# ConvNeXt-V2 block on one core: the expansion 13 instead of 14 slots behind the convolution

## The chip, the core and the metric

The kernel runs on one core of a Trainium2 chip. The core has five engines with a queue of instructions each: TensorE (PE, with its weight loads shown as PEld), VectorE (DVE), ScalarE (ACT), GpSimd (POOL) and SyncE (SP), which here only issues DMAs. Each queue is worked off in order; engines wait for one another by semaphores. The metric is the time of one execution in microseconds on the device. The time before is 1430.02 us, the median of three runs (1429.26 to 1431.42).

## What is computed

One block of a vision network on an image of 512 x 512 pixels and 96 channels, bfloat16:

```python
out = sum over i, j of xp[:, i:i+H, j:j+W, :] * dw[i, j]     # 3 x 3 depthwise convolution
h = layernorm(out)                                           # over the 96 channels of a pixel
h = gelu(einsum('bhwc,ce->bhwe', h, w1))                     # 96 -> 384: the expansion
gx = sqrt((h * h).sum(axis=(1, 2)) + 1e-6)                   # per channel, over the whole image
nx = gx / (gx.mean(axis=-1) + 1e-6)
h = grn_gamma * (h * nx) + grn_beta + h
return x + einsum('bhwe,ec->bhwc', h, w2)                    # 384 -> 96
```

The sum of squares in `gx` needs the whole image before the last product can begin. So there are two phases: the first makes the sums, the second the output.

## The kernel before

The image is cut into 128 blocks of four rows. The first phase runs in slots; `put` (line 842) enters in a table what is done for which block in which slot, and the loop from line 884 issues each slot's work engine by engine, in an order written out by hand. All engines used here are wrapped so that they keep the program's order (`InOrder`, line 26).

In slot s the block s is convolved: 72 small matmuls on PE in three bursts (`conv_taps`), which read x transposed by DVE (`turn_x`, three slots ahead) from tiles that SP loads five slots ahead (`load_x`, four buffers). ACT copies the result to `y_bf` (`evac`), DVE a third of it in some slots ("shared"). A square `ysq` follows (`stage_sq`, on POOL where the slot has an expansion, on ACT where it has none), and in slot s + 2 PE sums both over the channels (`stage_stats`).

Layer norm's factor is made for batches of four blocks. With L the slot of the last sums of a batch: `stage_moments` (DVE) in L scales the sums and clears them with a memset; `stage_rstd` (four small POOL operations) in L + 1; `stage_newton` (six more) and `stage_turn` (a DVE transposition of the result) in L + 2; `stage_rows` (two DMAs to DRAM) in L + 3; `stage_bcast` (four DMAs of 128 KB from there to all partitions, tile `rbc`) in L + 4. From slot L + 5 on one block a slot is multiplied (`stage_norm`, POOL, tile `yn`, three buffers). If the norm is in slot s, the four DMAs of `stage_write` to DRAM are issued in s + 1, the read back in another layout (`stage_read`, tile `ynT`) in s + 2, and the expansion is in s + 4: matmuls with w1, gelu on ACT into `g`, and the sum of squares, for some quarters by DVE (`bn_stats`, function `entry`), for the others by PE as a gram matrix (`gram_next`). The gram matrix and the sums of `stage_stats` share one PSUM bank.

The expansion of a block thus lies 14 slots behind its convolution. Slots 0 to 4, 7 and 10 to 17 have a convolution and no expansion, slots 18 to 127 have both, and slots 128 to 141 have an expansion alone (`mlp_tail`, 14 blocks from `TAIL0` on). 36 blocks are "whole": their `g` is stored to DRAM in three parts (`store_next`, one part a slot). Eight are held in SBUF for the second phase, in `gpool` or in tiles that the convolution no longer needs (`IN_XT`, `IN_XIN`, `IN_GH`). The rest are expanded a second time in the second phase (from line 1116), which multiplies by w2, adds x and writes the output.

SP's order within a slot from slot 20 on (lines 887 to 908): load of x, rows, broadcast, reads, writes, one store of `g`. POOL's: Newton steps, square, norm, rstd (lines 909 to 916).

Of the kernel before, what the change touches and what calls it, by code (L numbers as in the profile page):

```python
# [17 lines left out]
FILL = (6, 15)  # L18
BATCH = 4
WHOLE = (0, 3, 7)  # L20
NTAIL = 14
GRB = 3
PORTION = 4

# [33 lines left out]
def kernel(  # L58
# [30 lines left out]
    r_dram = dram.tile([NBLK, GR, W], bf16, name="r_dram")  # L89

    TAIL0 = NBLK - NTAIL
    HELD = [TAIL0 + i for i in (2, 3, 4, 6, 7, 9, 10, 11)]
    KEPT = [NBLK - 6, NBLK - 2, NBLK - 1]
    IN_XT, IN_XIN, IN_GH = (TAIL0, TAIL0 + 4), TAIL0 + 9, TAIL0 + 11

    def is_held(q):
        return q in HELD

    def is_whole(q):
        return q < TAIL0 and q % 10 in WHOLE or q == TAIL0  # L100

    def after_whole(q):
        return (q - 1) % 10 in WHOLE
# [99 lines left out]
    with ExitStack() as p1:  # L203
# [352 lines left out]
        def stage_moments(k):  # L556
            N = BATCHES[k][1] * GR * NG
            m = small.tile([128, 2, NS], f32, name="mom")
            dve.tensor_scalar(out=m[:, :, :N], in0=S[:, :, :N], scalar1=1.0 / C, scalar2=None, op0=ALU.mult)
            dve.memset(S[:], 0.0)  # L560
            msts[k] = m
# [134 lines left out]
        def quarter(b, t):  # L696
            return gs[b][t] if isinstance(gs[b], list) else gs[b][:, t]
# [9 lines left out]
        def mlp_tail(b, get):  # L707
            if b == IN_GH:
                gs[b] = late.gh.tile([128, NQ, NCH, QW], bf16, name="gh")[:]
            elif b > IN_GH:  # L710
                gs[b] = late.gr.tile([128, NQ, NCH, QW], bf16, name="gr")[:]
            elif b in IN_XT:
                gs[b] = g_xt
            elif b == IN_XIN:
                gs[b] = g_xin
            elif not is_held(b):
                while len(sums_only) < 2 * NQ:
                    sums_only.append(ypool.tile([128, NCH, QW], bf16, name="y_bf")[:])
                gs[b] = sums_only[:NQ]
                sums_only.extend(sums_only[:NQ])  # L720
                del sums_only[:NQ]
            else:
                gs[b] = gpool.tile([128, NQ, NCH, QW], bf16, name="g")[:]
            for t in range(NQ):
                cm = t < cm_quads(b)
                (cm_unit if cm else px_unit)(quarter(b, t), ynts[b], t)
                gram_next(12 if len(grams) > 24 else 6)
                if cm:
                    for j in range(NCH):
                        entry(b, j, t)  # L730
                if t == 1:
                    for k in get("turn"):
                        stage_turn(k)
                if t == 2:
                    for b2 in get("stats"):
                        stage_stats(b2)
                if t > cm_quads(b):
                    owe_grams(b, (t - 1) * QC, t * QC)
            for k in get("moments"):
                stage_moments(k)  # L740
            if cm_quads(b) < NQ:
                owe_grams(b, (NQ - 1) * QC, NQ * QC)
            if is_whole(b):
                stores.extend((b, h) for h in range(3))
# [63 lines left out]
        def gram_next(n):  # L808
            for b, c0, j in grams[:n]:
                c = c0 % QC + j * 128  # L810
                v = quarter(b, c0 // QC).rearrange("p j w -> p (j w)")[:, c:c + 128]
                pe.matmul(gram[:, j, :], lhsT=v, rhs=v, start=False, stop=True, skip_group_check=True)
            del grams[:n]
# [28 lines left out]
        def put(s, what, v):  # L842
            at.setdefault((s, what), []).append(v)

        RAMP = 4
        AHEAD = 20
        HOLE = 10
        LATE = 26
        last_norm = -1
        mlp_slots = set()  # L850
        for k, (b0, n) in enumerate(BATCHES):
            for b in range(b0, b0 + n):
                on_act = b not in mlp_slots
                put(b if on_act else b + 1, "sqa" if on_act else "sqp", b)
                last_s = b + 1 if b < RAMP else b + 2
                put(last_s, "stats", b)
            ramp = b0 + n <= RAMP
            if ramp:
                put(last_s, "chain", k)
                put(last_s + 1, "spread", k)  # L860
            else:
                put(last_s, "moments", k)
                put(last_s + 1, "rstd", k)
                put(last_s + 2, "newton", k)
                put(last_s + 2, "turn", k)
                put(last_s + 3, "rows", k)
                put(last_s + 4, "bcast", k)
            for b in range(b0, b0 + n):
                last_norm = s = max(last_norm + 1, last_s + (1 if ramp else 5))
                put(s, "norma" if ramp else "norm", b)  # L870
                put(s + 1, "write", b)
                put(s + 2, "read", b)
                m = s + (3 if ramp else 4)
                mlp_slots.add(m)
                put(m, "mlp", b)
                put(m + is_whole(b), "combine", b)
                last_slot = m
# [5 lines left out]
        turn_x(2)  # L883
        for s in range(last_slot + 1):
            get = lambda kind: at.get((s, kind), [])
            early = s < AHEAD
            if s < HOLE:
                for b in get("read"):
                    stage_read(b)
            while loaded[0] < min(s + 6, NBLK):  # L890
                load_x(loaded[0])
                loaded[0] += 1
            if HOLE <= s and early:
                for b in get("read"):
                    stage_read(b)
            for k in get("rows"):
                stage_rows(k)
            for k in get("bcast"):
                stage_bcast(k)
            if not early:  # L900
                for b in get("read"):
                    stage_read(b)
            for b in get("write"):
                stage_write(b)
            if not HOLE <= s < HOLE + 8:
                store_next()
            if any(b >= TAIL0 for b in get("mlp")):
                store_next()
            for k in get("newton"):
                stage_newton(k, pool)  # L910
            for b in get("sqp"):
                stage_sq(b, False)
            for b in get("norm"):
                stage_norm(b)
            for k in get("rstd"):
                stage_rstd(k, pool)
            mlp = get("mlp")

            def spread_out(bank=0):
                for k in get("spread"):  # L920
# [1 line left out]
                for b in get("norma"):  # L922
                    stage_norm(b, dve if b < 2 else pool)

            spare = not mlp and s % 2 == 1
            taps, evac = conv_taps(s, spare) if s < NBLK else ([], None)
            if mlp and mlp[0] >= TAIL0:
                assert not taps
# [36 lines left out]
            else:  # L965
                b = mlp[0]
# [32 lines left out]
                if not shared:  # L999
                    squares(2)  # L1000
                    gram_next(PORTION)
                if s >= LATE:
                    for k in get("turn"):
                        stage_turn(k)
                conv(2, u4)
                if evac:
                    evac(shared)
# [16 lines left out]
                    stage_moments(k)  # L1024
                squares_rest(2)
                square_owed()
                if s < LATE:
                    for k in get("turn"):
                        stage_turn(k)
                if is_whole(b):  # L1030
                    owed.append(lambda f=squares_rest: f(3))
                owe_grams(b, cm_quads(b) * QC, NQ * QC)
                if is_whole(b):
                    stores.extend((b, h) for h in range(3))
            if s == 0:
                setup_ynt()
            if s == 4:
# [129 lines left out]
```

## Time and profile before

The page of the profiled execution and the answers of its trace give:

| | us |
|---|---|
| profiled execution | 1432.47 |
| its span | 1429.7 |
| median of the three timed runs | 1430.02 |
| busy: ACT | 1379.6 (96%) |
| busy: PE | 1377.3 (96%) |
| busy: DVE | 1306.8 (91%) |
| busy: POOL | 888.8 (62%) |
| last evacuation of a convolution | at 857.83 |
| first instruction of the second phase's outputs on DVE | at 944.87 |

How to read it: the share over the whole span is an average over two phases with different work. POOL, for instance, has nothing but DMA issues in the second phase and is busy most of the first. So the stretches are read one by one. In a line of the timeline the columns are start, duration (of a merged group: from the first start to the last end), engine, line, operation, output and input tile, count, and in brackets the idle time before it with what ended it. All instructions that a wrapped engine issues have line 36 of the kernel, so they are told apart by their tiles. "SPq" is SP's queue of DMA issues; such an instruction ends when the DMA is issued, not when it has landed.

### The profile page before, as it was taken

The page shows a single profiled execution, that of the slowest core. Times are in us where ns is not written, and L with a number is a line of the kernel's source. Part 1 is how long each engine was busy: PE and PEld are TensorE (multiplying, and loading weights), DVE is VectorE, ACT ScalarE, POOL GpSimd, SP SyncE. Part 2 cuts the span into 40 slices and gives each one's busy share as a digit, 9 for nine tenths or more (in the row PEclk, how much of TensorE's full clock was granted, in tenths as well). Part 3 has the DMA queues.
Part 4 walks back from the last instruction along what each step waited for, and adds up shares of the span by engine and source line. Part 5 has one row for each costly group of instructions (what it writes and reads, how often), then busy time and mean ns, then how long its engine had stood idle before and what let it go on. Part 6 is the DMA issues. An engine that isn't in the chain of part 4 may idle for free.

```text
span 1429.7 us, 55018 instructions
## 1 busy us (share of the span) xinstructions
PE 1377.3 (96%) x23332; PEld 826.7 (58%) x23332; DVE 1306.8 (91%) x2400; ACT 1379.6 (96%) x1693; POOL 888.8 (62%) x735
## 2 busy tenths in 40 slices
PE   8989999999999999999999997799999999999998
PEld 3444555545555555555545554367777777777776
DVE  8958999999999999999999999988888888888888
ACT  7889999999999999999999999999999999999997
POOL 3559999999999999999999997302111111111110
PEclk9999999999999999999999999999999999999999
DMA  6568999898988998889888978649999999999996
GB/s 177 189 175 259 272 277 279 264 292 240 271 262 276 274 283 264 276 261 272 250 263 270 260 229 261 204 161 405 419 378 389 403 414 389 408 393 415 412 405 259
DMA packets 167565, 423.65 MB, mean 296 GB/s; under 512 B 34166, under 2 KB 83766, under 8 KB 162710
## 3 DMA queue, kind: packets, MB, share of 16 engines
q1 hardware_dynamic: 151652, 314.59, 68.9%
q0 software_dynamic: 15104, 105.39, 18.5%
q8 instruction: 182, 2.98, 0.9%
q14 instruction: 65, 0.53, 0.1%
q10 hardware_dynamic: 562, 0.15, 0.1%
HBM read 262.16 MB, written 157.79 MB: 294 GB/s over the span
## 4 chain that ended last, share of the span: by engine, by line
PE 51%; ACT 19%; DVE 17%; DMA 7%; issue 2%; SPq 2%; POOL 1%; ACTq 0%; POOLq 0%; DVEq 0%
PE PS L36 51%; ACT g L36 14%; DVE bst L36 10%; ACT y_bf L36 4%; DVE xT L36 3%; DVE o_sb L36 2%; DMA out_dram<-o_sb 2%; DMA yn_dram<-yn 2%; SPq L36 2%; DMA ynT<-yn_dram 1%; DMA xin<-in_x_dram 1%; DVE y_bf L36 1%; DMA rbc<-r_dram 1%; POOL ysq L36 1%; ACT xT L36 1%
## 5 line engine op out<-in xcount | busy, mean ns | idle before, releaser
L36 ACT ACTIVATE g<-PS 128x512 bf16<-128x512 f32 (+2 forms) x1160 | 703.7, 777 | 6.5 <-PE PS L36 6.1
L36 DVE BATCH_NORM_STATS2 bst<-g 128x6 f32<-128x512 bf16 x1020 | 623.4, 675 | 23.1 <-ACT g L36 22.3
L36 ACT ACTIVATE gr<-PS 128x1536 bf16<-128x1536 f32 x344 | 479.8, 1457 | 14.8 <-PE PS L36 8.6
L36 POOL TENSOR_TENSOR yn<-y_bf,rbc 128x1536 bf16<-128x1536 bf16 x126 | 391.6, 3110 | 55.5 <-DMA rbc<-r_dram 22.3
L36 PE MATMUL PS<-ynT,w1p 128*128 128x512 bf16 x1110 | 341.1, 380 | 22.1 <-ACT g L36 7.7
L36 PE MATMUL PS<-xT,Wq 64*32 64x511 bf16 (+1 forms) x9198 | 336.3, 386 | 7.8 <-ACT y_bf L36 1.0
L36 DVE TENSOR_TENSOR o_sb<-PS,B2c 128x384 bf16<-128x384 f32 x512 | 280.6, 556 | 58.8 <-PE PS L36 53.1
L36 POOL TENSOR_TENSOR ysq<-y_bf 128x1536 bf16<-128x1536 bf16 x114 | 313.4, 2750 | 25.0 <-ACT y_bf L36 17.7
L36 PEld LDWEIGHTS <-g 128*128 128x128 bf16 (+1 forms) x3603 | 217.5, 98 | 117.9 <-issue 35.4
L36 PE MATMUL PS<-ynT,w1s 128*128 128x512 bf16 x972 | 262.6, 379 | 0.2 <-issue 0.2
L295 POOL DMA_DIRECT2D xr<-in_x_dram x116 | 62.4, 538 | 286.4 <-DVE o_sb L36 286.4
L36 PEld LDWEIGHTS <-gr 128*128 128x128 bf16 x4104 | 200.9, 98 | 53.6 <-issue 1.8
L36 PE MATMUL PS<-W2s,gr 128*128 128x96 bf16 x4032 | 209.7, 206 | 1.0 <-DVE o_sb L36 0.4
L36 ACT ACTIVATE y_bf<-PS 128x1536 bf16<-128x1536 f32 (+2 forms) x147 | 182.5, 1264 | 14.1 <-PE PS L36 13.0
L36 PEld LDWEIGHTS <-w1p 128*128 128x128 bf16 x1110 | 94.8, 97 | 163.7 <-issue 109.7
L36 DVE STREAM_TRANSPOSE xT<-xin 128x576 f32<-128x576 f32 (+1 forms) x256 | 181.8, 751 | 6.1 <-PE PS L36 6.1
L36 PEld LDWEIGHTS <-Wq 64*32 64x32 bf16 x9216 | 104.6, 90 | 127.0 <-ACT g L36 56.5
L36 PE MATMUL PS<-g 128*128 128x128 bf16 x1632 | 157.8, 219 | 3.8 <-DVE PS L36 3.2
L36 DVE TENSOR_TENSOR o_sb<-o_sb,xr 128x768 bf16<-128x768 bf16 x256 | 142.8, 558 | 8.9
L36 PE MATMUL PS<-w1p,ynT 128*128 128x384 bf16 (+1 forms) x924 | 141.6, 273 | 7.4 <-ACT xT L36 2.1
L36 PEld LDWEIGHTS <-ynT 128*128 128x128 bf16 x924 | 73.0, 97 | 59.5 <-issue 37.1
L36 PE MATMUL PS<-W2s,g 128*128 128x96 bf16 x1968 | 103.9, 206 | 0.7 <-DVE o_sb L36 0.4
(114 smaller groups left out, 659.8 us busy)
## 6 DMA issues: line engine op xcount, KB each, us to landing
g<-g_dram POOLq DMA_DIRECT2D x36, 1536.0 KB, 9.8
xin<-in_x_dram SPq DMA_DIRECT2D x126, 432.0 KB
g_dram<-g SPq DMA_DIRECT2D x105, 512.0 KB
yn_dram<-yn SPq DMA_DIRECT2D x512, 96.0 KB
ynT<-yn_dram SPq DMA_DIRECT2D x128, 384.0 KB
out_dram<-o_sb SPq DMA_DIRECT2D x127, 384.0 KB
xr<-in_x_dram POOLq DMA_DIRECT2D x124, 384.0 KB, 7.5
ynT<-yn_dram SPq DMA_DIRECT2D x243, 128.0 KB
```

Of the source, the lines that this page charges most:

```text
L36: r = f(*a, **k)
L295: pq.dma_start(out=xr[:], in_=x[0, r0:r0 + GR].rearrange("r w c -> (r w) c").rearrange("(p g) c -> p g c", g=PXP))
```

## The change

The expansion of a block moves one slot nearer to its convolution. The steps between are put closer together, and several orders within a slot change with it:

- `NTAIL` is 13: the tail begins at block 115, slot 17 has an expansion, and there are 141 slots instead of 142. Block 114 stays whole; its `g` is now in `gpool` instead of the x tiles. The set of held blocks is unchanged.
- rstd, Newton steps, the transposition and the rows are all in slot L + 1, the broadcast in L + 2, the norm from L + 4 on. On POOL, in a slot that has all three, the order is norm, rstd with Newton steps, square; else square, rstd, norm. The transposition and the rows are issued at the slot's end.
- `yn` is written in the slot of its norm and read in the next one. The expansion is still four slots after the norm.
- SP's order in a slot becomes: load of x, reads, broadcast, store of `g`, and behind the norm the writes, then at the end the rows. The slots without a store end at 16 instead of 17.
- In the tail the transposition is at the slot's end instead of behind the second quarter; in the slot with the last moments the sums and the moments come behind the first quarter's matmuls, ahead of its `bn_stats`.
- In the slots from 10 on that have a convolution alone, the even ones instead of the odd ones use the spare banks.

```diff
-NTAIL = 14
+NTAIL = 13
...
-    HELD = [TAIL0 + i for i in (2, 3, 4, 6, 7, 9, 10, 11)]
+    HELD = [TAIL0 + i for i in (1, 2, 3, 5, 6, 8, 9, 10)]
...
-        return q < TAIL0 and q % 10 in WHOLE or q == TAIL0
+        return q < TAIL0 and q % 10 in WHOLE or q == TAIL0 - 1
...
                 (cm_unit if cm else px_unit)(quarter(b, t), ynts[b], t)
+                if t == 0 and get("moments"):
+                    for b2 in get("stats"):
+                        stage_stats(b2)
+                    for k in get("moments"):
+                        stage_moments(k)
...
-                if t == 1:
-                    for k in get("turn"):
-                        stage_turn(k)
-                if t == 2:
+                if t == 2 and not get("moments"):
...
-            for k in get("moments"):
-                stage_moments(k)
+            for k in get("turn"):
+                stage_turn(k)
...
                 put(last_s, "moments", k)
                 put(last_s + 1, "rstd", k)
-                put(last_s + 2, "newton", k)
-                put(last_s + 2, "turn", k)
-                put(last_s + 3, "rows", k)
-                put(last_s + 4, "bcast", k)
+                put(last_s + 1, "turn", k)
+                put(last_s + 1, "rows", k)
+                put(last_s + 2, "bcast", k)
             for b in range(b0, b0 + n):
-                last_norm = s = max(last_norm + 1, last_s + (1 if ramp else 5))
+                last_norm = s = max(last_norm + 1, last_s + (1 if ramp else 4))
                 put(s, "norma" if ramp else "norm", b)
-                put(s + 1, "write", b)
-                put(s + 2, "read", b)
+                put(s + ramp, "write", b)
+                put(s + ramp + 1, "read", b)
...
-            if HOLE <= s and early:
+            if HOLE <= s:
                 for b in get("read"):
                     stage_read(b)
-            for k in get("rows"):
-                stage_rows(k)
             for k in get("bcast"):
                 stage_bcast(k)
-            if not early:
-                for b in get("read"):
-                    stage_read(b)
-            for b in get("write"):
-                stage_write(b)
-            if not HOLE <= s < HOLE + 8:
+            if not HOLE <= s < HOLE + 7:
                 store_next()
             if any(b >= TAIL0 for b in get("mlp")):
                 store_next()
-            for k in get("newton"):
-                stage_newton(k, pool)
-            for b in get("sqp"):
-                stage_sq(b, False)
-            for b in get("norm"):
-                stage_norm(b)
-            for k in get("rstd"):
-                stage_rstd(k, pool)
             mlp = get("mlp")
+            steps = [lambda b=b: stage_sq(b, False) for b in get("sqp")]
+            norms = [lambda b=b: stage_norm(b) for b in get("norm")]
+            roots = [lambda k=k: (stage_rstd(k, pool), stage_newton(k, pool)) for k in get("rstd")]
+            for f in norms + roots + steps if roots and steps and norms else steps + roots + norms:
+                f()
+            for b in get("write"):
+                stage_write(b)
...
-            spare = not mlp and s % 2 == 1
+            spare = not mlp and s % 2 == (1 if s < HOLE else 0)
...
-                if s < LATE:
-                    for k in get("turn"):
-                        stage_turn(k)
+                for k in get("turn"):
+                    stage_turn(k)
...
+            for k in get("rows"):
+                stage_rows(k)
```

More of the change, by code (lines that the diff above doesn't have):

```diff
@@ L91 @@
     TAIL0 = NBLK - NTAIL
-    HELD = [TAIL0 + i for i in (2, 3, 4, 6, 7, 9, 10, 11)]
+    HELD = [TAIL0 + i for i in (1, 2, 3, 5, 6, 8, 9, 10)]
     KEPT = [NBLK - 6, NBLK - 2, NBLK - 1]
-    IN_XT, IN_XIN, IN_GH = (TAIL0, TAIL0 + 4), TAIL0 + 9, TAIL0 + 11
+    IN_XT, IN_XIN, IN_GH = TAIL0 + 3, TAIL0 + 8, TAIL0 + 10
     def is_held(q):
@@ L711, in mlp_tail @@
                 gs[b] = late.gr.tile([128, NQ, NCH, QW], bf16, name="gr")[:]
-            elif b in IN_XT:
+            elif b == IN_XT:
                 gs[b] = g_xt
@@ L845 @@
         RAMP = 4
-        AHEAD = 20
         HOLE = 10
-        LATE = 26
         last_norm = -1
@@ L885 @@
             get = lambda kind: at.get((s, kind), [])
-            early = s < AHEAD
             if s < HOLE:
@@ L1001 @@
                     gram_next(PORTION)
-                if s >= LATE:
-                    for k in get("turn"):
-                        stage_turn(k)
                 conv(2, u4)
@@ L1026 @@
                 square_owed()
-                if s < LATE:
-                    for k in get("turn"):
-                        stage_turn(k)
+                for k in get("turn"):
+                    stage_turn(k)
                 if is_whole(b):
```

## The prediction

> **What bounds the kernel now.** I read the page first, for the busy shares in its 40 slices, then the table of windows, then the waits and the timeline of SP's own DMA queue, because what is moved here is mostly DMA issues.
>
> ```profile
> span 1429.7 us, 55018 instructions
> ...
> ACT  7889999999999999999999999999999999999997
> ```
>
> The slices show one flat stretch, up to about 860 us, in which the convolution of one block and the expansion of an earlier one share a slot. The table of windows says how full it is; its columns are busy us of PE, PEld, DVE, ACT and POOL, clock, DMA share and GB/s.
>
> ```profile
> 200.00:850.00 650.00, 642.88 (x11798) 333.77 (x11796) 636.88 (x1123) 647.75 (x1033) 618.42 (x421) 1.00 0.89 266
> 900.00:925.00 25.00, 17.75 (x117) 9.26 (x117) 23.22 (x40) 25.00 (x20) 6.92 (x3) 1.00 0.59 177
> ```
>
> ACT is busy 647.75 of 650 us, so it sets the pace. On its timeline the evacuation of block 32 starts at 198.96 and that of block 120 at 809.70: 88 slots of 6.94 us, 27.76 us for the four slots of a batch. The others stand close behind. SP is not in that table, and its waits are where I look next: between 200 and 850 us,
>
> ```profile
> SPq L36 <- DMA yn_dram<-yn: 88.3, 116, 3.2
> ```
>
> SP waits for the landing of its own writes of yn: the read of a block may be issued only when that block's four writes are in DRAM. Two loops from SP's timeline (start, duration), the first a plain one, the second with the broadcast of rstd:
>
> ```profile
> 435.83 0.32 SPq L36 DMA_DIRECT2D ynT<-yn_dram  x1
> 436.60 2.52 SPq L36 DMA_DIRECT2D yn_dram<-yn  x4
> 439.16 1.35 SPq L36 DMA_DIRECT2D g_dram<-g  x1
> 440.62 0.37 SPq L36 DMA_DIRECT2D xin<-in_x_dram  x1
> 442.11 0.33 SPq L36 DMA_DIRECT2D ynT<-yn_dram  x1
> ```
>
> ```profile
> 475.06 0.33 SPq L36 DMA_DIRECT2D ynT<-yn_dram  x1
> 475.45 2.58 SPq L36 DMA_DIRECT2D yn_dram<-yn  x4
> 478.13 0.53 SPq L36 DMA_DIRECT2D g_dram<-g  x1
> 478.70 0.44 SPq L36 DMA_DIRECT2D xin<-in_x_dram  x1
> 479.19 2.64 SPq L36 DMA_DIRECT2D rbc<-r_dram  x4
> 481.94 0.36 SPq L36 DMA_DIRECT2D ynT<-yn_dram  x1
> ```
>
> The reader is to see the order: read, writes, store of g, load of x, broadcast, next read. The store, the load and the broadcast stand between the writes and the read that waits for them. In the first loop the read comes 2.99 us after the writes' last issue, 1.12 us of it idle; in the second 3.91 us of issues cover the landing. Over this stretch the plain loops take 6.80 us (read to read, 40 of them), those with a broadcast 7.21, those with the rows of rstd 6.77. A batch is two plain ones and one of each: 27.6 us. SP hardly waits for anything else, so it runs at ACT's pace with nothing to spare.
>
> **The change part by part.** The profiled execution took 1432.47 us, 2.8 us more than its span and 2.45 above the median of 1430.02. I work out differences on its rows and put them on the median.
>
> *One slot fewer.* Slot 17, a convolution alone, takes over the expansion of block 4, and that of block 114 goes from the tail into slot 127. A slot with a convolution alone costs 3.49 us (evacuations at 66.90 and 91.30, seven slots); an expansion alone in the tail 5.38 (fourteen on ACT from 861.04 to 936.40); both together 6.94. Sum: 6.94 - 3.49 - 5.38 = -1.9 us. The square of block 17 goes to POOL (2.75 us; POOL has gaps there, the largest 8.4 us before 102.68).
>
> *rstd whole in one slot.* No instruction is added. POOL's order becomes norm, ten small operations, two squares; before, one square stood in front of the norm. Its four slots cost 4 x 3.07 + 4 x 2.70 + 3.9 = 27.0 us either way, under 27.76. rstd is ready 2.7 us sooner against its slot; the transposition of it is asked for up to a slot sooner, so DVE can wait for POOL there, and behind it stand the transpositions of x and the casts. It did so before, 2.82 us at 85.16 and 1.89 at 109.72. In the steady stretch the evacuation of a slot plus about 1 us is where I put rstd, plus 2.6 us where DVE gets to it: no wait. In the first two batches I allow 2 to 6 us of DVE time, which lies beside ACT work: 0 taken, 4 us as the upper end.
>
> *Rows and broadcast sooner.* The same DMAs. POOL's wait for the broadcast goes, but POOL is not the bound: 0, at best the 3.0 us of ACT waits between 98 and 135 us, for reads that came late after the hole. I take -1.5.
>
> *yn written in its norm's slot, the store ahead of it.* This is the large term. SP's order becomes load of x, read, broadcast, store of g, four writes, rows. Between writes and the read that waits for them only the load of x is left (and the rows in one slot of four); store and broadcast now follow that wait instead of covering it. The chain from read to read is then serial:
>
> - read 0.33 + 0.08 to the next issue = 0.41;
> - store 0.70 + 0.08 = 0.78, in nine slots of ten;
> - writes 2.51 + 0.08 = 2.59;
> - from the writes' last issue to the next read 3.31 (mean of the 40 plain loops, 1.76 to 5.01), which hides the load of x, and the rows' 1.3 us as well.
>
> A plain slot is 7.09 us, one with a broadcast 2.1 more. Four slots: 4 x 7.09 + 2.1 - 0.3 for missing stores = 30.2 us against ACT's 27.76. The landing may get shorter when transfers spread out. The nearest row with less traffic is in the tail, where the DMA share is 0.59 (second window above):
>
> ```profile
> 906.93 2.48 SPq L36 DMA_DIRECT2D yn_dram<-yn  x4
> 911.10 0.31 SPq L36 DMA_DIRECT2D ynT<-yn_dram  x1
> ```
>
> 1.69 us there, 2.07 in the next loop: about 1.9 at 0.59 and 3.31 at 0.89. On a line between them the new share, 0.89 x 27.76/29.4 = 0.84, gives 3.1 us and a batch of 29.4 us. That is 0.41 us a slot too slow. The chain breaks even at a landing of 2.7 us. How an order of this kind runs is seen once before, in slots 17 and 18, where read and broadcast stand ahead of the writes:
>
> ```profile
> 94.29 0.33 SPq L36 DMA_DIRECT2D ynT<-yn_dram  x1
> 94.67 1.82 SPq L36 DMA_DIRECT2D rbc<-r_dram  x4
> 96.53 5.52 SPq L36 DMA_DIRECT2D yn_dram<-yn  x4
> 102.15 0.53 SPq L36 DMA_DIRECT2D xin<-in_x_dram  x1
> 103.90 0.31 SPq L36 DMA_DIRECT2D ynT<-yn_dram  x1
> ```
>
> 9.6 us for a loop without a store, so 9.2 for one with a broadcast is not too high.
>
> The lag is absorbed at first: block 60 is read at 475.06 and expanded from about 486.4 (seven gelus before the evacuation at 490.61), 11.3 us later, of which I leave 4 to the read itself. So 7 us are free, 17 slots at 0.41. From slot 18 to the last load of x in slot 122 there are 105: 88 x 0.41 = +36 us. In the tail SP's loops without load and store (4.5 to 5.3 us) keep up with ACT's 5.38: 0. What is late first is the read of yn, then PE's first matmuls of an expansion, then ACT.
>
> The Trainium skill, *DMA: Bandwidth & Descriptors*, section "Latency and other measured facts", says the receipt from HBM makes most of a DMA's fixed cost, 0.2 us on average and 2 us at high load, less when the load is lighter. The trace agrees in direction (1.69 and 3.31 us). By that rule alone, an estimate, up to 1.8 us of landing could go, and the 36 us would be 0; by the rows they are 36.
>
> *The tail.* Moments ahead of bn_stats, the transposition of rstd at the slot's end. ACT runs from 861.04 to 936.40 without a gap and covers all of it; without that cover it is the 0.5 us of moments and memset. 0 taken. *Where the moments fall.* An expansion is one block further on at each moments slot, and the gram matmuls that waited for the memset (0.90 us at 181.04, six waits of 3.7 us in all) fall elsewhere: -4 to +4, 0 taken.
>
> Sum: -1.9 - 1.5 + 36 + 0 = +33 us, 2.3%: 1430 + 33 = 1463.
>
> **The rivals.**
>
> *Faster: the landing shrinks below 2.7 us.* Its place is SP's wait between the writes and the read. For it: 1.7 to 2.1 us in the tail, and the minimum of 1.76 among the plain loops; SP then never gets 7 us behind. Against: between 824 and 860 us, where no x is loaded any more and the share is 0.81 to 0.82, it is 3.83, 3.33, 1.85 and 2.62 in the four loops without rows or broadcast, 2.9 in the mean. Then only the first terms stay: -1.9 - 1.5, and up to -4 for the gram waits: 1423 to 1428, say 1426. By the rule cited above this one would win; the rows at 0.81 and above speak against that.
>
> *Heavier: the landing stays at 3.31 or the writes wait as at 96.53.* With 30.2 to 31 us a batch: 0.6 to 0.8 us a slot over some 95 slots, +57 to +76, less 3.4: 1484 to 1503.
>
> *No change: SP keeps up, and what the slot gives is taken back by DVE* waiting for rstd after the hole, 4 us at most since DVE then sets ACT back only once: 1427 to 1432, say 1430. The 2.82 us at 85.16 speak for it, DVE's 13 us of slack between 200 and 850 against.
>
> **How the numbers follow.** Chances: the serial chain as worked out 0.55 (landing 2.85 to 3.25 us, 28.4 to 30 us a batch, 1436 to 1483); heavier 0.13; faster 0.22; no change 0.10, of which 0.08 within 0.2% and 0.02 slower. 0.2% is about what a measurement of this kernel can tell from no change. So faster 0.22, same 0.08, slower 0.70. The point is the likeliest case's, 1463. The range leaves out a tenth at each end, the lower half of the faster case and most of the heavier one: 1425 to 1490; the likeliest case's own is 1436 to 1483.
>
> **What would show it.** In SP's timeline of after: read, store, writes, load, read, with a gap of 2 us and more ahead of the reads where there was 1.75; loops of 7 us and more, over 9 with a broadcast; evacuations on ACT more than 7.2 us apart from about slot 35 on, with PE waiting for the read of yn and ACT for PE; ACT's busy share in the stretch down to some 94% and the DMA share to 0.84. It is wrong if ACT stays at 99% there, if the landing falls to 2.7 us or less, or if SP waits for POOL's norm instead. POOL's wait for the broadcast should be gone in any case.

## The result and the profile after

The changed kernel takes 1528.57 us (median of five runs, 1527.89 to 1533.31), the kernel before 1429.26 us beside it (1426.69 to 1431.42): a ratio of 1.0704, 95% interval 1.0685 to 1.0723. It is 99 us slower; 33 were forecast, and the range ended at 1490. Slower was right, and so was the place, but the time lost is three times the sum.

The first two lines below are the span and ACT's slices on the page of the changed kernel, the next two its table of windows, with the same columns as that of before (busy us of PE, PEld, DVE, ACT and POOL, clock, DMA share, GB/s):

```profile
span 1526.2 us, 55022 instructions
...
ACT  7879989899889989998998899799999999999997
```

```profile
200.00:850.00 650.00, 591.33 (x10555) 303.73 (x10553) 573.76 (x1004) 589.13 (x922) 549.45 (x376) 0.97 0.81 239
946.00:1026.00 80.00, 55.20 (x437) 31.05 (x422) 61.98 (x113) 67.66 (x52) 40.07 (x24) 0.89 0.68 206
```

ACT is busy 589.13 of 650 us, 91%, where it was 647.75. No engine is full any more, and the DMA share has fallen from 0.89 to 0.81: something waits in a circle. From the evacuation of block 32 (210.0) to that of block 120 (893.1) a batch of four slots takes 31.05 us instead of 27.76. The second line is the tail, where ACT had no gap before; now it stands still for 12.3 us.

The waits of SP's queue and of all engines, 200 to 850 us:

```profile
SPq L36 <- DMA yn_dram<-yn: 148.6, 171, 4.1
SPq L36 <- DMA ynT<-yn_dram: 15.7, 15, 2.3
```

```profile
POOL yn L36 <- DMA rbc<-r_dram: 82.4, 21, 5.9
ACT g L36 <- PE PS L36: 58.8, 80, 2.8
DVE xT L36 <- DMA xin<-in_x_dram: 48.9, 35, 3.5
PEld L36 <- DMA ynT<-yn_dram: 47.5, 40, 3.1
```

SP waits 148.6 us for the landing of its own writes (88.3 before), and the engines wait for what SP issues: POOL for the broadcast, DVE for x, PE for the read of yn, ACT for PE. SP waits only 4.6 us for POOL's norm. The second line of SP's waits, 15.7 us for reads to land, is taken up in the last section. Two loops of SP's timeline, one with a broadcast and one plain:

```profile
492.22 0.33 SPq L36 DMA_DIRECT2D ynT<-yn_dram  x1
492.61 1.81 SPq L36 DMA_DIRECT2D rbc<-r_dram  x4
494.46 0.42 SPq L36 DMA_DIRECT2D g_dram<-g  x1
494.93 5.27 SPq L36 DMA_DIRECT2D yn_dram<-yn  x4
500.24 0.59 SPq L36 DMA_DIRECT2D xin<-in_x_dram  x1
501.98 0.33 SPq L36 DMA_DIRECT2D ynT<-yn_dram  x1
502.40 0.38 SPq L36 DMA_DIRECT2D g_dram<-g  x1
502.87 3.36 SPq L36 DMA_DIRECT2D yn_dram<-yn  x4
506.27 0.59 SPq L36 DMA_DIRECT2D xin<-in_x_dram  x1
509.99 0.33 SPq L36 DMA_DIRECT2D ynT<-yn_dram  x1
```

The order is the one that was forecast. The writes take 5.27 and 3.36 us, not 2.51. Means of SP's loops that have a load of x and a store, between 200 and 850 us, read to read, worked out from the timelines (the writes from the first issue's start to the last one's end):

| | plain | with broadcast | with rows |
|---|---|---|---|
| before: loop / writes / writes to next read | 6.80 / 3.07 / 3.31 | 7.21 / 2.63 / 4.17 | 6.77 / 2.61 / 3.75 |
| after: loop / writes / writes to next read | 7.44 / 3.31 / 3.15 | 9.74 / 3.87 / 2.85 | 7.00 / 3.20 / 2.78 |

### The profile page after: what moved, and what is told of

Its sections match the earlier page's. It is cut to its first block, busy times and chain, and to the rows that moved or that the text cites. A ratio compares the mean times of both kernels' runs of the same rounds, so it can differ in the third digit from the quotient of the medians.

```text
span 1526.2 us, 55022 instructions
## 1 busy us (share of the span) xinstructions
PE 1406.4 (92%) x23332; PEld 836.2 (55%) x23332; DVE 1310.6 (86%) x2400; ACT 1392.4 (91%) x1698; POOL 890.2 (58%) x736
## 4 chain that ended last, share of the span: by engine, by line
PE 42%; DMA 19%; DVE 14%; POOL 10%; SPq 7%; ACT 5%; issue 3%; POOLq 0%; ACTq 0%; DVEq 0%
PE PS L36 42%; DVE bst L36 9%; DMA yn_dram<-yn 7%; SPq L36 7%; DMA ynT<-yn_dram 5%; POOL yn L36 4%; DMA xin<-in_x_dram 4%; ACT g L36 3%; POOL ysq L36 3%; DVE xT L36 3%; DMA rbc<-r_dram 3%; ACT y_bf L36 1%; POOL var L36 1%; POOL rn L36 1%; DVE y_bf L36 1%
## 5 line engine op out<-in xcount | busy, mean ns | idle before, releaser
L36 ACT ACTIVATE g<-PS 128x512 bf16<-128x512 f32 (+2 forms) x1170 | 718.4, 736 | 82.0 <-PE PS L36 78.8
L36 PE MATMUL PS<-ynT,w1p 128*128 128x512 bf16 x1110 | 351.2, 391 | 49.9 <-DMA ynT<-yn_dram 36.3
L36 PE MATMUL PS<-xT,Wq 64*32 64x511 bf16 (+1 forms) x9198 | 346.5, 392 | 9.8 <-issue 2.3
L36 PEld LDWEIGHTS <-g 128*128 128x128 bf16 (+1 forms) x3603 | 220.9, 99 | 146.3 <-issue 66.5
L36 ACT ACTIVATE y_bf<-PS 128x1536 bf16<-128x1536 f32 (+1 forms) x147 | 179.9, 1235 | 20.5 <-PE PS L36 20.0
L36 PE MATMUL PS<-g 128*128 128x128 bf16 x1632 | 162.4, 223 | 28.0 <-DVE PS L36 27.6
L36 PE MATMUL PS<-w1p,ynT 128*128 128x384 bf16 (+1 forms) x924 | 147.5, 281 | 9.7 <-DMA ynT<-yn_dram 5.7
```

Of the source, the lines that this page charges most:

```text
L36: r = f(*a, **k)
```

## The experiments

Theory A is the prediction's: SP's order of issues makes a serial chain from read to read, and that sets the pace. Rival B: the new slots of rstd, rows and broadcast cost the time; POOL's 82.4 us of waits for the broadcast speak for it. Rival C: the write in its norm's slot makes SP wait for POOL.

**Which part of the change it is**

*e3: the kernel before with nothing changed but SP's order.*

```diff
-            for k in get("rows"):
-                stage_rows(k)
-            for k in get("bcast"):
-                stage_bcast(k)
+            if early:
+                for k in get("rows"):
+                    stage_rows(k)
+                for k in get("bcast"):
+                    stage_bcast(k)
             if not early:
                 for b in get("read"):
                     stage_read(b)
+                for k in get("bcast"):
+                    stage_bcast(k)
+                store_next()
             for b in get("write"):
                 stage_write(b)
+            if not early:
+                for k in get("rows"):
+                    stage_rows(k)
-            if not HOLE <= s < HOLE + 8:
+            if early and not HOLE <= s < HOLE + 8:
                 store_next()
...
```

> The kernel before (14 slots, everything in its old slot), but from slot 20 on with the changed kernel's order on SP: load of x, read, broadcast, store, writes, rows. Theory A: the same serial chain as in the changed kernel, 30.5 to 31 us a batch from slot 20 on: 1500 to 1530. Rivals B and C: nothing of rstd or of the norm's slot is touched, 1428 to 1435.

It took 1518.85 us, ratio 1.0597 (1.0572 to 1.0622), 30.79 us a batch. The order alone, with 14 slots and rstd where it was, costs 89 of the 99 us. The waits of all engines, 200 to 850 us:

```profile
POOL yn L36 <- DMA rbc<-r_dram: 70.5, 20, 5.7
```

POOL's wait for the broadcast is there too, though the broadcast's slot was not touched. It is a result of SP's lateness, not a cause, and rival B falls: e4 below, with the broadcast at the changed kernel's place, has no such wait at all.

*e8: the changed kernel with SP's order of before, and the write one slot behind its norm.* All other parts of the change stay.

```diff
-                put(last_s + 1, "rows", k)
-                put(last_s + 2, "bcast", k)
+                put(last_s + 2, "rows", k)
+                put(last_s + 3, "bcast", k)
...
-                put(s + ramp, "write", b)
-                put(s + ramp + 1, "read", b)
+                put(s + 1, "write", b)
+                put(s + 2, "read", b)
...
```

The rest of the edit puts the slot in this order: load of x, rows, broadcast, reads, writes, store, then POOL's work.

> The version with SP's order of before in 13 slots (load of x, rows, broadcast, read, writes, store), but the write one slot behind its norm and the read two, as before. That version took 1496 us, with SP waiting 84 us for POOL's norm. If the norm's slot for the write is what made it slow (rival C, for that order): SP's waits for POOL's norm gone, 27.7 to 28 us a batch, 1426 to 1438. If the rows and the broadcast in that order are what made it slow: 1480 and more still.

It took 1428.79 us, ratio 0.9985 (0.9969 to 1.0002), 27.69 us a batch. So all the rest, one slot fewer, rstd in one slot, rows and broadcast sooner, the tail, is worth nothing that the measurement can tell from zero. (The broadcast comes one slot sooner than before here, in the changed kernel two.) ACT is full again:

```profile
200.00:850.00 650.00, 644.23 (x11850) 334.34 (x11848) 637.09 (x1124) 648.86 (x1035) 617.93 (x423) 1.00 0.89 268
```

*e9: the changed kernel with only the write a slot later.* This is the fourth corner: SP's order of after, the write's slot of before.

```diff
-                put(s + ramp, "write", b)
-                put(s + ramp + 1, "read", b)
+                put(s + 1, "write", b)
+                put(s + 2, "read", b)
...
+            for b in get("write"):
+                stage_write(b)
             mlp = get("mlp")
...
-            for b in get("write"):
-                stage_write(b)
```

> The changed kernel's order on SP (load of x, read, broadcast, store, writes, rows) with 13 slots, but each write one slot behind its norm and each read two, as before: the fourth corner beside the changed kernel (this order, write in the norm's slot: 1529 us), SP's order of before with the write in its norm's slot (1496) and SP's order of before with the write a slot later (1429). Theory A (store and broadcast ahead of the writes make the serial chain): as the same order in the kernel before, 30.6 to 31 us a batch, 1510 to 1525. Rival C (the norm's slot for the write is what costs): 1428 to 1440.

1520.27 us, 1.0626 (1.0587 to 1.0665), 30.84 us a batch, as theory A said. From e8 to e9 the order, with rows and broadcast back in the changed kernel's slots, costs 91.5 us; from e9 to the changed kernel the norm's slot adds 8.3.

*e2: SP's order of before, but the write in its norm's slot.* It is e8 without the later write:

```diff
-                put(last_s + 1, "rows", k)
-                put(last_s + 2, "bcast", k)
+                put(last_s + 2, "rows", k)
+                put(last_s + 3, "bcast", k)
...
```

The rest of the edit gives this order: load of x, rows, broadcast, reads, then POOL's work, writes, store.

> The changed kernel (13 slots, rstd in one slot, write in its norm's slot, moments ahead of bn_stats), but with SP's order of before: load of x, rows, broadcast, read, writes, store; the rows are issued at the start of the next slot and the broadcast one slot later, both still a slot nearer to the convolution than in the kernel before. Theory A: loops of 6.8 to 7.2 us again, ACT sets the pace, 1422 to 1432, POOL's wait for the broadcast and PE's for the read all but gone, and the granted clock of the mixed stretch back at 1.00. Rival B (rstd, its transposition and the moments in their slots): at least 1490. Rival C (SP waits for POOL's norm, since the write still stands in its norm's slot): at least 1460.

Theory A alone failed here: 1495.68 us, 1.0446 (1.0409 to 1.0483), 30.04 us a batch. SP's waits and, below them, POOL's timeline of one batch:

```profile
SPq L36 <- POOL yn L36: 83.7, 38, 4.3
SPq L36 <- DMA yn_dram<-yn: 68.2, 95, 3.1
```

```profile
408.45 6.18 POOL L36 TENSOR_TENSOR yn<-y_bf,rbc 128x1536 bf16<-128x1536 bf16 x2 [2.94 <-DMA rbc<-r_dram]
...
418.47 5.45 POOL L36 TENSOR_TENSOR ysq<-y_bf 128x1536 bf16<-128x1536 bf16 x2
423.88 3.11 POOL L36 TENSOR_TENSOR yn<-y_bf,rbc 128x1536 bf16<-128x1536 bf16 x1
```

POOL makes two norms in a row, then rstd and two squares, and the next norm starts 9.25 us after the second one's end (414.63 to 423.88). A write in its norm's slot has nothing between it and that norm, so SP waits for it, and POOL in turn waits for SP's broadcast. With the write a slot later (e8) SP waits 1.2 us for POOL's norm in the same stretch. Rival C is thus true, for this order: either part of the change, the order or the write's slot, is enough to make it slow (+91.5 and +66.9 against e8), and the two together cost 99.8, not their sum.

*e6: the changed kernel with store and broadcast both behind the writes.*

```diff
-            for k in get("bcast"):
-                stage_bcast(k)
-            if not HOLE <= s < HOLE + 7:
-                store_next()
...
             for b in get("write"):
                 stage_write(b)
+            if not HOLE <= s < HOLE + 7:
+                store_next()
...
+            for k in get("bcast"):
+                stage_bcast(k)
```

> The changed kernel with both the store and the broadcast behind the writes: load of x, read, writes, store, broadcast, rows. Theory A: no loop is long any more (with a broadcast about 6.8 us in place of 8.90 with the store alone moved), 27.7 to 27.8 us a batch, ACT sets the pace; 4 us less than with the store alone: 1434 to 1438. What stays above the kernel before is then the stretch of slots 10 to 20, where the first expansions wait. Rival C (the write in its norm's slot makes SP wait for POOL as soon as the broadcast comes later): over 1445, with SP waiting for POOL's norm.

1455.62 us, 1.0182 (1.0134 to 1.0230): rival C again, and not theory A. SP waits 41.1 us for POOL's norm; the later broadcast makes the norm late, and the write hangs on the norm.

**What in the order costs the time**

*e4: the changed kernel, each read one slot later,* so that a whole loop lies between a block's writes and its read.

```diff
-                put(s + ramp + 1, "read", b)
+                put(s + 2, "read", b)
```

> The changed kernel with each block's read one slot later, so that a whole loop of SP lies between a block's writes and its read; order of SP and all else as changed. Theory A: the wait for the landing, 2.1 to 2.5 us a loop, is gone, loops could run in some 5.5 us plain and 7.7 with a broadcast, ACT sets the pace again: 1422 to 1432. Rival B: at least 1490. Rival C: unchanged, 1520 to 1532.

1436.25 us, 1.0043 (1.0023 to 1.0063), 27.71 us a batch. A plain loop takes 5.98 us, and SP's waits for the landing of yn have gone from 148.6 us to 0.8 (waits of its queue, 200 to 850 us):

```profile
SPq L36 <- DMA yn_dram<-yn: 0.8, 2, 0.7
```

The window shows ACT full again, with store and broadcast still ahead of the writes:

```profile
200.00:850.00 650.00, 644.00 (x11842) 334.90 (x11826) 638.77 (x1126) 648.45 (x1034) 617.73 (x421) 1.00 0.90 267
```

So the wait for the landing closes the chain. What was missed is 4 to 5 us more than "1422 to 1432", and it lies at the start: the evacuation of block 17 comes at 104.1 us, in the changed kernel at 95.8.

*e7: the same, but blocks 4 to 7 read as in the changed kernel.*

```diff
-                put(s + ramp + 1, "read", b)
+                put(s + ramp + 1 if b < 8 else s + 2, "read", b)
```

> The changed kernel with the read one slot later from block 8 on alone; blocks 4 to 7 are read as in the changed kernel. If the 6 us that the version with all reads a slot later stands above the kernel before come from the first mixed slots (evacuation 17 at 104.1 us there, 95.8 in the changed kernel, 91.3 before): evacuation 17 at 95 to 97, steady batch 27.7, in all 1427 to 1433. If they come from the tail or elsewhere: 1434 to 1438 again.

1435.39 us, 1.0034 (1.0017 to 1.0050). Block 17 came at 98.1, but block 18 only at 109.4, as in the changed kernel (108.1; in e8 103.5). The lost time moved by one slot; the forecast of 1427 to 1433 missed.

*e1: the changed kernel with only the store moved behind the writes.*

```diff
-            if not HOLE <= s < HOLE + 7:
-                store_next()
-            if any(b >= TAIL0 for b in get("mlp")):
-                store_next()
...
             for b in get("write"):
                 stage_write(b)
+            if not HOLE <= s < HOLE + 7:
+                store_next()
+            if any(b >= TAIL0 for b in get("mlp")):
+                store_next()
```

> The changed kernel with one thing different: the store of g stands behind the four writes of yn, between them and the next read, and no longer ahead of them. Theory A (SP's own order of DMA issues sets the pace: what stands behind the wait for the landing is paid, what stands ahead of it is hidden): the store, 0.38 us and 0.08 to the next issue in the changed kernel's plain loops, is hidden again in about nine loops of ten: 1.7 us off a batch of 31.05, 22 batches and the slots before and behind them, about -40 us: 1480 to 1495. Rival B (what costs is rstd and its rows and broadcast in their new slots: POOL waits 86 us for the broadcast, DVE for rstd, gram matmuls for the memset): unchanged, 1525 to 1532. Rival C (the write in its norm's slot makes SP wait for POOL): unchanged, 1525 to 1532.

1440.71 us, 1.0071 (1.0043 to 1.0100), 27.93 us a batch: 39 us and more below the 1480 to 1495 that theory A gave. This one line of order is worth 88 us, twice what the issue of a store, 0.47 us a loop, can explain. The writes became faster with it: 2.77 us in plain loops (3.31), 3.41 with a broadcast (3.87).

*e5: the store in its place and as often, but an eighth of its bytes.*

```diff
-                sp.dma_start(out=g_dram[whole.index(b)][:, h * n:h * n + n],
-                             in_=flat(b)[:, h * n:h * n + n])
+                sp.dma_start(out=g_dram[whole.index(b)][:, h * n:h * n + n // 8],
+                             in_=flat(b)[:, h * n:h * n + n // 8])
```

> The changed kernel, store of g in its place ahead of the writes and just as often, but only an eighth of its columns is stored (64 KB of 512 KB), and the loads of the second phase read that eighth eight times over: most of g is left out, the output is not the reference's, and only the pace of the mixed slots is read from it (evacuation of block 32 to that of block 120, in the changed kernel 31.05 us a batch, with the store behind the writes 27.93). Theory A1 (what costs is the store's issue on SP, 0.38 to 0.47 us a loop, which stays here): 30.5 to 31.1 us a batch, writes still 3.2 to 3.9 us a loop. Theory A2 (what costs is mainly the store's bytes, which stand in SP's DMA queue ahead of the writes, so that the writes' issue stalls and their landing comes later): writes down to about 2.7 us plain, loops of 6.6 to 6.9, 28.3 to 29.3 us a batch.

This kernel leaves out seven eighths of the stored `g`, so only its pace counts. The pace is 27.75 us a batch, ACT's own, in a single execution (the 1447.71 us of the whole are not compared, since the second phase loads otherwise). Its window:

```profile
200.00:850.00 650.00, 643.11 (x11817) 333.84 (x11810) 637.23 (x1123) 647.76 (x1034) 614.48 (x420) 1.00 0.77 206
```

The issue is still there, 0.39 us, and costs nothing that ACT's pace shows; the 448 KB that are gone were the price. Plain writes take 2.91 us and the next read comes 2.61 us behind them: 0.94 us less than in the changed kernel for the two. In the changed kernel it is the second of the four writes that is slow to issue, 1.20 us in the mean of plain loops against 0.76 here and 0.67 in e1. In loops with a broadcast the writes stay at 3.86 us, so there the store's bytes are not what makes them long. In e1 all bytes are moved and only their place differs. The reading that fits both runs is that neither the store's issue nor its bytes as such cost the time, but its bytes just ahead of the writes.

*e11: the load of x (432 KB) between the store and the writes.*

```diff
-            while loaded[0] < min(s + 6, NBLK):
+            while s < HOLE + 10 and loaded[0] < min(s + 6, NBLK):
                 load_x(loaded[0])
                 loaded[0] += 1
...
+            while loaded[0] < min(s + 6, NBLK):
+                load_x(loaded[0])
+                loaded[0] += 1
             for b in get("write"):
                 stage_write(b)
```

> The changed kernel, from slot 20 on with the load of x (432 KB) between the store and the writes in place of behind the writes. Its issue of 0.6 us, hidden in the landing until now, comes into the serial chain, and so do its bytes. Theory A2 (bytes that stand in SP's queue ahead of the writes cost about what the store's 512 KB cost, 1.2 us a loop in all): 1.0 to 1.2 us a loop, 35 to 36 us a batch, 1615 to 1640. Issue alone: 0.5 to 0.6 us a loop, 33 to 33.5 us a batch, 1570 to 1585. If neither counts: 1525 to 1535.

1610.92 us, 1.1251 (1.1219 to 1.1283), 34.43 us a batch. That the loop grows by what is put ahead of the writes holds; that bytes cost alike does not quite: plain loops grew by 0.80 us (7.44 to 8.24), of which 0.58 is the issue of the load and the way to the next one. One loop:

```profile
512.40 0.33 SPq L36 DMA_DIRECT2D ynT<-yn_dram  x1
512.83 1.14 SPq L36 DMA_DIRECT2D g_dram<-g  x1
514.02 0.42 SPq L36 DMA_DIRECT2D xin<-in_x_dram  x1
514.54 2.96 SPq L36 DMA_DIRECT2D yn_dram<-yn  x4
520.31 0.33 SPq L36 DMA_DIRECT2D ynT<-yn_dram  x1
```

Nothing is left to cover the landing: 2.81 us of idle (517.50 to 520.31). A load of x ahead of the writes costs its issue and 0.2 us or so; a store of nearly the same size cost at least 0.8 us a loop beside its issue, since that much pace came back in e5. Why a store is dearer than a load there is open. The slow issue is again the second one behind the store: here that is the first write, 1.11 us, and the second is back at 0.65.

*e10: the store at its place, but from ACT's queue.*

```diff
-                sp.dma_start(out=g_dram[whole.index(b)][:, h * n:h * n + n],
+                act.dma_start(out=g_dram[whole.index(b)][:, h * n:h * n + n],
```

> The changed kernel with the store of g issued at the same place of the slot from ACT's DMA queue in place of SP's. All bytes stay, also their moment. If what the store costs is its bytes ahead of the writes in one and the same queue: loops of 6.3 to 6.6 us plain, 27.8 to 28.6 us a batch, 1435 to 1455 with what the issues take from ACT. If the bytes contend with the writes on whatever queue they come: writes still 3.2 us and more, landing 3 us, 29.5 to 31 us a batch, 1480 to 1530.

1484.89 us, 1.0371 (1.0331 to 1.0412), 29.49 us a batch: between the two, and not settled by this run, because ACT was held up itself. ACT's waits in 200 to 850 us:

```profile
ACT g L36 <- DMA yn_dram<-yn: 15.3, 8, 2.9
ACT g L36 <- PE PS L36: 12.3, 26, 1.0
ACT g L36 <- DMA rbc<-r_dram: 7.4, 2, 4.2
ACT g L36 <- DMA ynT<-yn_dram: 5.4, 2, 4.6
```

Its gelus wait behind its DMA issues, which wait for landings of SP's DMAs: the trace shows the stores on ACT taking their turn among the same eight semaphores as SP's DMAs (last section). The store at 212.17 us, for instance, waited for a write that SP had issued at 208.74. With no store in SP's queue the plain writes still took 2.99 us and the read came 3.27 us behind them (2.91 and 2.61 in e5). The Trainium skill, *DMA: Bandwidth & Descriptors*, section "Issuing engines are not separate DMA queues", says that DMAs run on the same 16 DMA engines whatever engine issues them; the landing, 3.27 us and no shorter than with the store in SP's own queue (3.15), agrees.

**The tail**

*e12: e8 with the moments of the tail at the end of their slot again, as before.*

```diff
-                if t == 0 and get("moments"):
-                    for b2 in get("stats"):
-                        stage_stats(b2)
-                    for k in get("moments"):
-                        stage_moments(k)
...
+            for k in get("moments"):
+                stage_moments(k)
             for k in get("turn"):
```

> The version with SP's order of before, 13 slots and the write a slot behind its norm (1429 us), and in the tail the moments at the end of their slot again, as in the kernel before, so that the gram matmuls behind them don't wait for the memset in the first unit of an expansion. In that version ACT waits 0.9 us once in the tail, behind 0.6 us of PE's wait for the memset, and nowhere in the kernel before. If the tail's order costs that: 0.5 to 1.5 us less, 1427 to 1428.5, just under the kernel before; if the wait is covered or comes back elsewhere: 1428 to 1430.

Wrong in sign: 1432.29 us, 1.0017 (1.0004 to 1.0031), 3.5 us more than e8. Its waits, 860 to 882 us:

```profile
ACT g L36 <- PE PS L36: 4.5, 1, 4.5
PE PS L36 <- DVE PS L36: 4.2, 1, 4.2
```

The moments and their memset then stand behind twelve `bn_stats` on DVE (869.77 to 876.98), and PE's gram matmuls wait 4.2 us for the memset. In the tail of 13 slots the change's new order is needed; it costs 0.9 us of ACT's time instead of 4.5.

No version beats the kernel before: e8 is level with it, all others are slower.

## Why the prediction was right and wrong

*What is late.* Right: SP's chain, then the read of yn, then PE, then ACT, with ACT at 91% (94% forecast) and the DMA share at 0.81 (0.84). e3, e4 and e9 show the cause by putting the order in, opening the chain, and leaving all but the order.

*The writes, 2.59 us.* This is the first step that failed. The duration, 2.51, was read from loops like the two that are shown (2.52 and 2.58); the mean of the 40 plain ones was 3.07 and stood in the same trace, while the landing was taken from that mean. After the change it was 3.31 in plain loops, 3.87 with a broadcast and 3.20 with rows. Put into the sum alone, these add 3.3 us to a batch; shorter stores and landings and the loops without a store take about half of it back. The mean of 3.07 would have come nearer, but in part by luck: 13 of the 40 loops have a wait of the third write in it, and the other 27 average 2.70. After the change no plain loop has that wait; there the second write takes 1.20 us instead of 0.72. e5 and e1 point to the reason: the store's bytes now stand right ahead of the writes. In the loops with a broadcast it is mainly another: the third write waits 0.78 us in the mean, for the landing of the read. The line at 96.53 us showed writes of 5.52 us behind read and broadcast, and the prediction used that loop only to accept 9.2 us, and gave the case that writes wait 0.13.

*The other terms of the loop.* Each with the way to the next issue: read 0.41: 0.43. Store 0.78: 0.55 in the mean of plain loops. Landing 3.1 to 3.3: 3.15. Broadcast 2.1: 2.06. A plain loop is 0.43 + 0.55 + 3.31 + 3.15 = 7.44, against 6.88 forecast with a landing of 3.1; one with a broadcast 9.74. The batch is 31.05 us, 29.4 forecast (the terms as written give 29.3, and 34 us instead of 36): 0.82 us a slot too slow instead of 0.41. That is double, and 36 us more over 88 slots.

*The landing's share.* It shrank by 0.16 us in plain loops while the DMA share went from 0.89 to 0.81; the line between 1.9 us at 0.59 and 3.31 at 0.89 gives 0.38 for that. By the rule cited in the prediction (the Trainium skill, *DMA: Bandwidth & Descriptors*, "Latency and other measured facts") up to 1.8 us could have gone, an estimate; the trace shows less than a tenth of that at this load.

*The 17 slots that absorb the lag.* Mostly wrong. Against e8, which has the same slots, the changed kernel's evacuations are late by:

| block | 20 | 32 | 120 | 127 | end of span |
|---|---|---|---|---|---|
| us late | 4.7 | 8.2 | 82.0 | 87.4 | 99.0 |

Between 20 and 32 it loses 0.29 us a slot instead of 0.84, so a part of the lag is absorbed there, but 4.7 us were lost before slot 20 already, in the first mixed slots: PE's gram matmuls wait 2.9 us for the memset of the moments, which DVE reaches late, and the evacuation of block 18 comes 12.3 us after that of block 17 (7.7 in e8).

*The tail, 0.* Wrong: 11.6 us. "SP's loops without load and store (4.5 to 5.3 us)" overlooked that the first slots of the tail still store, two of them two parts each, and that the stores, like the broadcasts, now stand ahead of the writes. One such loop in SP's timeline of the changed kernel:

```profile
966.45 0.31 SPq L36 DMA_DIRECT2D ynT<-yn_dram  x1
966.85 0.85 SPq L36 DMA_DIRECT2D g_dram<-g  x2
967.80 4.10 SPq L36 DMA_DIRECT2D yn_dram<-yn  x4
973.95 0.33 SPq L36 DMA_DIRECT2D ynT<-yn_dram  x1
```

7.5 us, where ACT needs 5.38. Only from 995.39 on, without stores, do the loops take 4.6 to 5.4 us, as forecast. So 73.8 of the 99 us come from the slots 32 to 120, where 36 were forecast for nearly the same stretch; the rest from the start, the absorption and the tail, which stood at nothing.

*One slot fewer, rstd, rows and broadcast: -1.9, 0 and -1.5.* e8 has them, with the broadcast one slot sooner instead of two. Its ratio gives -2.1 us, with an interval of -4.4 to +0.3, so -3.4 is inside it. That POOL's wait for the broadcast "should be gone in any case" was wrong, as it hung on SP being in time: 82.4 us, and none in e8.

*The rivals.* "Heavier", 30.2 to 31 us a batch, was the case that came (31.05); its 1484 to 1503 lacked the start and the tail. "Faster" fell on the landing, as the rows had it. The case that SP waits for POOL's norm was named among what would prove the prediction wrong: in the changed kernel it is 4.6 us, since SP's chain is the slower of the two, but e2 and e6 show it right behind.

## What to carry to other kernels

A queue that waits for its own landing is priced as a loop: what stands between the write and the dependent issue is free up to the landing, what stands behind it is paid in full, and a store of 512 KB right ahead of the writes cost more here than its issue, at least 0.8 us a loop beside it. Take the durations for such a sum from a loop with the same neighbours, and a mean only after looking at which waits are in it. Count the DMAs in a queue too: where eight semaphores go round, each one waits for the eighth before it. A transfer issued in the slot of the instruction that it waits for couples two queues with no slack between them; put a slot between, and the same work ran at full pace.

## What was not expected of the hardware

The granted clock fell below 1 although TensorE had less to do: its mean is 0.978 over the changed kernel, 0.949 in e11, 0.999 in e8 and before. The table of windows of the changed kernel shows it following a pause:

```profile
380.00:384.00 4.00, 1.39 (x32) 0.57 (x31) 4.00 (x7) 1.98 (x4) 3.50 (x8) 0.92 0.73 257
384.00:388.00 4.00, 4.00 (x39) 1.66 (x40) 4.00 (x9) 2.52 (x5) 3.75 (x6) 0.65 0.75 172
```

PE is busy 1.39 of 4 us, and in the next 4 us it runs at 0.65. The Trainium skill, *TensorE: Matmul & The Clock Gate*, "Part 1: The HAM clock gate", has the clock throttled after an idle window of about 3.4 us; the trace agrees in kind, though the longest gap between matmuls from 200 to 850 us is 2.63 us, so a shorter pause was enough. The low clock follows from the waits here: with the chain opened (e4, e5, e8) the stretch is at 1.00 again. What it costs in its turn was not measured.

An issue on SP is not a fixed price: the second write took 0.67 to 1.20 us in the mean of plain loops, by what stood ahead of it.

The third write's wait of 0.78 us in loops with a broadcast, until the read of that loop had landed, is the program's own. The DMAs of SP use eight semaphores in turn: in the trace of the changed kernel each one between 200 and 850 us signals the semaphore of the eighth before it (696 of 696), and it waits until that one has landed. A read, four DMAs of the broadcast, the store and two writes make the third write the eighth behind the read. In e1, with the store out of the way, the eighth is the fourth write, and there the wait (0.73 us) moved to the fourth. The same count fits the kernel before, where in the plain loop that follows a broadcast the third write is the eighth behind a load of x (SP's waits, 200 to 850 us, before):

```profile
SPq L36 <- DMA xin<-in_x_dram: 21.5, 17, 2.8
```

So it is a wait that the order of the DMAs sets, and it can be counted ahead. A limit of the queue itself is not shown by it.
